# New buffers for gathered rows and one-hot tiles in a fused attention and expert kernel

## The chip, the cores and the metric
The kernel runs on one core of one Trainium2 chip. The metric is the device time of one execution in microseconds (us). The engines are named as the profile names them: PE (matmuls; PEld is its weight load), DVE (vector engine), ACT (scalar engine), POOL (GpSimd), SP (which issues DMAs). Each has its own instruction stream and works it off in order; a wait at the head of a stream holds all that stands behind it.

## The reference
Three stages follow each other. The first is an attention over 32 pooled memory slots per head; its output is read as 4608 tokens of 512 numbers. The second sends each token to one of eight experts of at most 576 tokens, taken greedily by the size of the logit, and applies that expert's two layers. The third is a dense layer pair on all tokens.

```python
a = softmax(phi over the sequence)             # 8 batches, 8 heads, 576 tokens, 32 slots
k_m, v_m = a.T @ k, a.T @ v
x = softmax(q @ k_m.T / 8) @ v_m               # -> 4608 x 512
assigned = greedy(argsort(-(x @ w_gate)), capacity=576)
for e in range(8):
    mask = assigned == e
    out[mask] = relu(x[mask] @ w1[e]) @ w2[e]  # 512 -> 1024 -> 512
h = out @ w_in                                 # 512 -> 2048
y = (h * clip(h + 3, 0, 6) / 6) @ w_out        # 2048 -> 512
```

## The kernel before
**Numbers in halves.** Matmuls run on 16-bit floats. Each factor is split into a high and a low part (scaled by a power of two), and each product is three matmuls. ACT makes the high part, DVE or POOL the low one. The scale needs the largest value over all partitions, which `all_max` finds by a matmul against the identity (tile `amx`, line 694).

**The stages on PE.** After attention, `for P in range(4)` runs `l1(2P)`, `l2(2P)`, `l1(2P+1)`, `l2(2P+1)`, `l34(P)`: the two layers of two experts, and then the dense pair on both experts' 1152 tokens. In `l1` a pass makes a 128-row block of the hidden layer; for expert 0 a pass takes two blocks, 48 matmuls, and there are four passes. `l34` takes 3 chunks of 384 tokens; per chunk it makes 16 hidden tiles (`p<-yt,wi`, 12 matmuls each) and adds 16 products (`acc<-wo,h`, 9 matmuls each), two tiles behind; a group of the latter waits for the `h<-h,p` instruction of its tile on DVE.

**Who fills the gaps.** The engines' orders are fixed when the program is built. A planner written in Python keeps a clock `CK` and estimated times of DVE, ACT and POOL. Background tasks are generators (`routes`, `weights`, `gathers`, `dense`, and the small `ev` tasks that empty a PSUM tile). Each `yield`s the time at which it wants to go on; after every matmul `run()` polls the tasks that are due. `need(cond)` lets the clock run on until a condition holds. So an edit in one task can move instructions of all engines anywhere behind it.

**What the change touches.** `mm_slot` (line 631) deals out the PSUM slots: the list `MMQ` holds the last four, and a new tile waits for the oldest to be emptied. `routes` finds which tokens go to expert k; DVE compares indices into a one-hot tile `OH` of six blocks, six times per expert, and PE multiplies each by `RH` (line 951, `rtp<-RH,OH`, 36 matmuls); the token list `ix` comes out of it. `gathers` fetches an expert's tokens in five blocks `xg` by indirect DMAs on POOL, has PE transpose them (line 623, `xp<-ident,xg`), and writes the two halves `xt`. `weights` loads a layer's weights in four blocks `wst` (indirect DMAs on POOL), finds their scale (the trace prints its maximum as `s_0m` for expert 0 and `s_1m` for expert 1, without the layer; the one at 275.62 us is of the second layer), and splits them: eight instructions each on ACT and DVE (`w<-wst,s,w`). `dense` converts the dense weights, which come as 64-bit floats, in 32 pieces; each takes four DVE instructions on a buffer `cva` (three with two inputs, one with one), some ACT work and one POOL subtraction (`wi<-cva,wi` or `wo<-cva,wo`). `spare` lends these pieces the buffers that nobody uses at the time. The scale of a finished expert's output is `sy_0m` or `sy_1m`.

Of the kernel before, what the change touches and what calls it, by code (L numbers as in the profile page):

```python
# [9 lines left out]
F32 = mybir.dt.float32  # L10
F16 = mybir.dt.float16
BF16 = mybir.dt.bfloat16
# [8 lines left out]
def attn_moe_kernel(ctx: ExitStack, tc: tile.TileContext, q, k, v, phi, w_gate, w1, w2, w_in, w_out, out):  # L21
    nc = tc.nc
    B, H, S, D = q.shape
    M = phi.shape[3]
    E = w_gate.shape[1]
    NT = 36
# [18 lines left out]
    ones_c = consts.tile([128, 128], F32)  # L45
# [44 lines left out]
    with tc.tile_pool(name="ald", bufs=2) as ald, tc.tile_pool(name="aw", bufs=2) as aw, \  # L90
# [3 lines left out]
        for i in range(2):  # L94
            t = slot(26 + i, [128, 4, 2, 64], F32, f"vna{i}")
# [349 lines left out]
        for t in range(-LEAD - 4 - PRE, NTK + A1 + 2):  # L445
# [72 lines left out]
            if t in DT:  # L518
                tag, m = DT[t]
                bufs, shape = (2, [128, 2, 4, R * D]) if tag == "kvt" else (3, [128, H, 4 * D])  # L520
# [25 lines left out]
    rt = ctx.enter_context(tc.tile_pool(name="rt", bufs=1))  # L546
# [33 lines left out]
    V_ = Eng(nc.vector, 0.1, 0.00105)  # L580
# [48 lines left out]
    MMQ = []  # L629

    def mm_slot(done):
        while len(MMQ) >= 4:
            d = MMQ.pop(0)
            b, CK.busy = CK.busy, False
            need(lambda: d[0])
            CK.busy = b
        MMQ.append(done)

    def mm_tile(shape, name, done):
# [22 lines left out]
    nc.vector.tensor_scalar(triu, jp, 0.0, None, op0=OP.is_lt)  # L662
    onesb = rt.tile([128, 128], BF16, name="onesb")
    nc.vector.memset(onesb, 1.0)
    ones72 = rt.tile([128, 2 * NT], F32, name="ones72")
    nc.vector.memset(ones72, 1.0)
    wE = rt.tile([128, E], F32, name="wE")
    nc.vector.tensor_scalar(wE, iT[:, 0:E], -1.0, float(E), op0=OP.mult, op1=OP.add)
    pb = rt.tile([128, 4], F32, name="pb")
# [67 lines left out]
    def route(k):  # L737
# [120 lines left out]
        else:  # L858
# [11 lines left out]
        V_.scalar_tensor_tensor(G[:, 0], V, thf, be, op0=OP.is_gt, op1=OP.mult)  # L870
        V_.scalar_tensor_tensor(G[:, 1], V, thf, be, op0=OP.is_equal, op1=OP.mult)
        sc = rt.tile([128, 2, NT], F32, name="scn")
        V_.tensor_tensor_scan(sc.rearrange("p a t -> p (a t)"), ones72, G.rearrange("p a t -> p (a t)"), 0.0,
                              op0=OP.mult, op1=OP.add)
        tot = rt.tile([128, 2], BF16, name="tot")
        V_.tensor_copy(tot, sc[:, :, NT - 1])
# [46 lines left out]
        p = ps.tile([128, 64], F32, name="rtp")  # L923

        def oh(q4):
            o = rt.tile([128, 6, 128], BF16, name="OH", bufs=3)
            V_.tensor_tensor(o, lo[:, 6 * q4:6 * q4 + 6, None].to_broadcast([128, 6, 128]),
                             i128[:, None, :].to_broadcast([128, 6, 128]), op=OP.is_equal)
            return o
# [53 lines left out]
    def weights():  # L983
        for T in range(2 * E):
            k, which = divmod(T, 2)
            while k not in EIX or T == 3 and 1 not in XI:
                yield CK.now + 0.3
            for c in range(4):
                if T == 0 and c == 2:
                    while not OHP[0]:  # L990
                        yield CK.now + 0.1
                w_issue(T, c)
                yield CK.now + 0.8, G_
            while not XD[0]:
                yield CK.now + 0.1
            sq = rt.tile([128, 4], F32, name="wsq", bufs=2)
            for c in range(4):
                st, ready = WST[T, c]
                yield ready, A_
                scr = wk.tile([128, 1024], BF16, name="wscr")  # L1000
                A_.activation(scr, st, AF.Square, accum_out=sq[:, c:c + 1])
                yield A_.t - 0.3
            s4 = rt.tile([128, 1], F32, name="ws4", bufs=2)
            yield A_.t + HOP
            while 0 not in IDX:
                yield CK.now + 0.1
            V_.tensor_reduce(s4, sq, axis=AX.X, op=OP.add)
            yield V_.t + HOP
            s = yield from pow2(s4, f"s{which}_{k}", True, 0, (4, 13)[which])
            (S1, S2)[which][k] = s  # L1010
            while k and (L1D, L2D)[which].get(k - 1, 0) < (8, 4)[which]:
                yield CK.now + 0.3
            tl, rd = [], []
            for n in range(9):
                if n < 8:
                    c, i = divmod(n, 2)
                    if i == 0:
                        tl.append(wk.tile([128, 2, 1024], F16, name=f"w{which}_{c}"))
                    cs = slice(i * 512, i * 512 + 512)
                    if n in PS.get(T, ()):  # L1020
                        A_.activation(WST[T, c][0][:, cs], WST[T, c][0][:, cs], AF.Copy, scale=s[:, 0:1])
                        yield A_.t - 0.3
                        A_.activation(tl[c][:, 0, cs], WST[T, c][0][:, cs], AF.Copy)
                    else:
                        A_.activation(tl[c][:, 0, cs], WST[T, c][0][:, cs], AF.Copy, scale=s[:, 0:1])
                    rd.append(A_.t + HOP)
                if n and n - 1 in PS.get(T, ()):
                    yield rd[n - 1], G_
                    c, i = divmod(n - 1, 2)
                    cs = slice(i * 512, i * 512 + 512)  # L1030
                    G_.tensor_tensor(tl[c][:, 1, cs], WST[T, c][0][:, cs], tl[c][:, 0, cs], op=OP.subtract)
                    yield CK.now + 0.1, A_
                    WC[T] = c + i, tl
                elif n:
                    yield rd[n - 1], V_
                    c, i = divmod(n - 1, 2)
                    cs = slice(i * 512, i * 512 + 512)
                    V_.scalar_tensor_tensor(tl[c][:, 1, cs], WST[T, c][0][:, cs], s[:, 0:1], tl[c][:, 0, cs],
                                            op0=OP.mult, op1=OP.subtract)
                    if i and T + 1 < 2 * E and T != 2:  # L1040
                        w_issue(T + 1, c)
                    yield CK.now + 0.1, A_
                    WC[T] = c + i, tl
            yield V_.t
            (W1, W2)[which][k] = tl

    XT, XI = {}, set()

    def ybuf(m):
        return wk.tile([128, CAP], F32, name=f"y_{m}")  # L1050
# [4 lines left out]
    def gathers():  # L1055
        for k in range(E):
# [7 lines left out]
            def fetch(i):  # L1064
                n = 64 if i == 4 and k % 2 == 0 else 128
                if k == 0:
                    xg = hbuf(3 + i)[:, 0:512]
                elif k == 1 and i > 1:
                    if i % 2 == 0:
                        big.append(wk.tile([128, 2, 512], F32, name="xg", tag=f"wst{i // 2 - 1}"))  # L1070
                    xg = big[-1][:, i % 2]
                else:
                    xg = wk.tile([128, 512], F32, name="xg", tag=f"xg{i % 2}")
                G_.indirect_dma_start(out=xg[:n], out_offset=None, in_=xd, in_offset=U(ap=ix[:n, i:i + 1], axis=0))
                rdy.append(dma(0.75, G_.t))
                xgs.append((i, n, xg))
            depth = 2 if k > 1 else 5
            big = []
            if k == 0:
                G_.t = max(G_.t, XDT[0])  # L1080
            for i in range(depth):
# [1 line left out]
                    while not SR[0]:  # L1083
                        yield CK.now + 0.1
                fetch(i)
            XI.add(k)
            while k and L1D.get(k - 1, 0) < 8:
                yield CK.now + 0.3
            xt = wk.tile([128, 2, 4, CAP], F16, name="xt")
# [56 lines left out]
    def spare(kind):  # L1146
        tags = ["dst0", "dst1", "dst2"] if kind else ["cva0", "cva1"]
        if 1 in XT or 1 in L1D:
            tags += [] if kind else ["xg0", "xg1"]
        if 1 in W2:  # L1150
            tags += [f"wst{c}" for c in range(4)] if kind else ["wscr"]
        for t in tags:
            if t not in BUSY:
                return t
# [379 lines left out]
```

## Time and profile before
| | us |
|---|---|
| three runs | 1522.28, 1525.7, 1526.74 (median 1525.7) |
| profiled execution | 1519.59 |
| its span | 1517.7 |
| PE busy | 1402.9 (92%) |
| DVE busy | 838.6 (55%) |
| ACT busy | 734.0 (48%) |
| POOL busy | 481.0 (32%) |

All rows below are of the profiled execution, whose own time lies 6.1 us under the median of the three runs. The attention stage takes the first part of the span. `l1(0)` starts at about 255 us, `l2(0)` at 294.04, `l1(1)` at 324.83, `l2(1)` at 350.94, the first `l34` at 381.20; after that PE is nearly always busy. Shares of the span hide this: DVE is busy 55% of the span and nearly all of the time in the stretch where the dense weights are converted.

### The profile page before, as it was taken

Reading aid. Unit: us, or ns where it says so; the run is one execution under the profiler, and the core shown is the slowest. Engines: PE = TensorE matmul, PEld = TensorE weight load, DVE = VectorE, ACT = ScalarE, POOL = GpSimd, SP = SyncE. Lnnn points to the kernel's source line nnn. Section 1 sums busy time; section 2 is a strip of 40 time slices with the busy share of each in tenths; the row PEclk is TensorE's granted clock in tenths of the full one; section 3 lists DMA queues with packets and bytes.
Section 4 is the critical chain, followed back from the end, with each engine's and each line's share of the span. In section 5 each row is a group of like instructions: output and inputs, shape, how many; then the busy total and the mean of one; then the engine's idle time right before and its main releaser. Section 6 shows DMA issues by size and latency. Waiting matters only on the chain.

```text
span 1517.7 us, 26287 instructions
## 1 busy us (share of the span) xinstructions
PE 1402.9 (92%) x10506; PEld 931.7 (61%) x10506; DVE 838.6 (55%) x1985; ACT 734.0 (48%) x1419; POOL 481.0 (32%) x557
## 2 busy tenths in 40 slices
PE   4778886898889999999999999999999999999997
PEld 3667765786444445897544458885545588855553
DVE  5788967899985973453158743522477335221111
ACT  3667655577763553453335533623346536233332
POOL 4555305134552533200224332102235311023232
PEclk9989996999999999999999999999999999999999
DMA  9865577355300420200003220200023102000000
GB/s 301 291 229 194 178 254 242 131 179 167 112 27 22 136 78 21 82 17 1 1 22 93 72 70 30 70 1 1 21 67 111 56 29 70 1 0 22 1 21 21
DMA packets 65913, 130.67 MB, mean 86 GB/s; under 512 B 5248, under 2 KB 35968, under 8 KB 65792
## 3 DMA queue, kind: packets, MB, share of 16 engines
q1 hardware_dynamic: 49808, 74.48, 14.9%
q0 software_dynamic: 15168, 52.96, 10.8%
q8 instruction: 82, 1.34, 0.4%
q10 hardware_dynamic: 816, 1.57, 0.3%
q14 instruction: 39, 0.32, 0.1%
HBM read 110.12 MB, written 18.87 MB: 85 GB/s over the span
## 4 chain that ended last, share of the span: by engine, by line
PE 64%; DVE 16%; issue 6%; ACT 6%; DMA 5%; POOL 3%; SPq 0%; ACTq 0%; POOLq 0%; DVEq 0%
PE p L618 37%; PE acc L618 19%; DVE cva L567 4%; PE xa L420 2%; DMA xg<-xd,ix 2%; DMA wst<-in_moe_w_dram,ei 2%; POOL h L567 1%; DVE h L567 1%; PE kvp L191 1%; PE rtp L794 1%; DMA kvt<-in_v_dram 1%; DVE OH L567 1%; ACT wscr L567 1%; ACT h L567 1%; DVE pm L138 1%
## 5 line engine op out<-in xcount | busy, mean ns | idle before, releaser
L618 PE MATMUL p<-yt,wi 128*128 128x384 f16 x2304 | 422.8, 327 | 0.0
L618 PE MATMUL acc<-wo,h 128*128 128x512 f16 x1728 | 418.0, 380 | 4.5 <-ACT h L567 4.0
L567 POOL TENSOR_TENSOR h<-h,h 128x384 f16<-128x384 f32 x192 | 183.7, 957 | 623.6 <-ACT h L567 449.6
L618 PEld LDWEIGHTS <-w 128*128 128x128 f16 x3072 | 339.6, 121 | 49.9 <-issue 4.3
L618 PEld LDWEIGHTS <-wi 128*128 128x128 f16 x2304 | 218.6, 98 | 155.7 <-issue 1.6
L567 DVE SCALAR_TENSOR_TENSOR h<-h,p 128x384 f32<-128x384 f32 x192 | 105.9, 551 | 332.6 <-ACT h L567 317.1
L567 ACT ACTIVATE h<-p,half_c,inv 128x384 f32<-128x384 f32 (+1 forms) x256 | 143.9, 587 | 301.2 <-PE p L618 293.3
L618 PEld LDWEIGHTS <-h 128*128 128x128 f16 x1728 | 163.7, 98 | 173.7 <-ACT h L567 5.6
L618 PE MATMUL p<-xt,w 128*128 128x288 f16 x1536 | 198.0, 288 | 3.7 <-DVE h L567 3.5
L618 PE MATMUL p<-h,w 128*128 128x288 f16 x1536 | 197.3, 288 | 4.3 <-DVE w L567 3.7
L567 ACT ACTIVATE h<-h 128x384 f16<-128x384 f32 x192 | 100.1, 521 | 117.8 <-DVE h L567 116.5
L567 POOL DMA_INDIRECT wst<-in_moe_w_dram,ei x64 | 66.2, 1035 | 110.2 <-DVE tot L567 33.8
L567 DVE SCALAR_TENSOR_TENSOR h<-p,h 128x288 f16<-128x288 f32 x128 | 57.3, 454 | 78.9 <-ACT h L567 78.9
L567 ACT ACTIVATE h<-p 128x288 f16<-128x288 f32 x128 | 52.1, 414 | 90.7 <-PE p L618 89.7
L567 DVE SCALAR_TENSOR_TENSOR w<-wst,s,w 128x512 f16<-128x512 f32 x124 | 94.5, 781 | 2.4 <-ACT w L567 2.4
L567 ACT ACTIVATE w<-wst,s 128x512 f16<-128x512 f32 x124 | 83.7, 715 | 8.5 <-DVE s L567 5.8
L567 DVE SCALAR_TENSOR_TENSOR cva<-dst,cva 128x512 int32<-128x512 int32 (+1 forms) x96 | 82.6, 881 | 0.4 <-ACT dst L567 0.2
L567 DVE TENSOR_REDUCE ym<-y 128x1 f32<-128x288 f32 x64 | 28.8, 450 | 93.8 <-ACT y L567 91.9
L567 ACT ACTIVATE wscr<-wst 128x1024 bf16<-128x1024 f32 x64 | 67.3, 1052 | 19.0 <-DMA wst<-in_moe_w_dram,ei 18.0
L567 ACT ACTIVATE y<-p 128x288 f32<-128x288 f32 x64 | 26.0, 406 | 96.3 <-PE p L618 92.8
L567 POOL DMA_INDIRECT xg<-xd,ix x35 | 36.4, 1040 | 75.1 <-PE xp L623 55.6
L191 PE MATMUL kvp<-kvt,A 128*64 128x128 f32 x576 | 44.6, 309 | 7.3 <-ACT A L170 3.0
(313 smaller groups left out, 1568.5 us busy)
## 6 DMA issues: line engine op xcount, KB each, us to landing
dst<-in_moe_w_out_dram SPq DMA_DIRECT2D x26, 512.0 KB, 3.6
qt<-in_q_dram SPq DMA_DIRECT2D x8, 1024.0 KB, 13.3
dq<-in_moe_w_in_dram SPq DMA_DIRECT2D x16, 512.0 KB, 4.9
xd<-xs SPq DMA_DIRECT2D x32, 256.0 KB, 5.1
kvt<-in_k_dram SPq DMA_DIRECT2D x7, 1152.0 KB, 5.4
kvt<-in_v_dram SPq DMA_DIRECT2D x7, 1152.0 KB, 12.4
dst<-in_moe_w_in_dram SPq DMA_DIRECT2D x15, 512.0 KB, 4.6
ph<-in_phi_dram SPq DMA_DIRECT2D x8, 576.0 KB, 11.0
```

Of the source, the lines that this page charges most:

```text
L138: nc.vector.tensor_reduce(pm, PH[b].rearrange("p h (r m) -> p h m r", m=M), axis=AX.X, op=OP.max)
L191: nc.tensor.matmul(p[i * 64:(i + 1) * 64, g, 0:128], A[:, hp, r, :], KV[b][:, :, hp, r * 64:(r + 1) * 64], start=(r == 0), stop=(r == R - 1))
L420: nc.tensor.matmul(p[r, g], AT[u][:, half, g, r], VB[b][:, g], start=True, stop=True)
L567: r = f(*a, **kw)
L618: nc.tensor.matmul(o, l, r, start=start, stop=stop)
L794: nc.tensor.matmul(p[:60, :32], C[:, 4 * t:4 * t + 4].rearrange("p t n -> p (t n)"), Bo[:, 4 * t:4 * t + 4].rearrange("p t e -> p (t e)"), ...
```

## The change
Five edits. `mm_slot` waits for the oldest slot first and takes it off the list afterwards; before, it took it off first and waited with three on the list, so that a background task's matmul could take the fourth. `OH` has two buffers instead of three, and a constant tile of ones that only the scan used goes. `xg` has three buffers of its own for all experts but the first; before it had two, and expert 1's third to fifth block lay in the weight buffers `wst0` and `wst1`. So `weights` no longer waits for expert 1's gathers (`XI`) and reloads its buffers at once there too (`T != 2`). The gathers run three blocks ahead for experts 2 to 7 (two before), and three for expert 1 (five before). `spare` may lend `xg2` as well.

```diff
--- before.py
+++ after.py
@@ -630,10 +630,12 @@
 
     def mm_slot(done):
         while len(MMQ) >= 4:
-            d = MMQ.pop(0)
+            d = MMQ[0]
             b, CK.busy = CK.busy, False
             need(lambda: d[0])
             CK.busy = b
+            if MMQ and MMQ[0] is d:
+                MMQ.pop(0)
         MMQ.append(done)
 
     def mm_tile(shape, name, done):
@@ -662,8 +664,6 @@
     nc.vector.tensor_scalar(triu, jp, 0.0, None, op0=OP.is_lt)
     onesb = rt.tile([128, 128], BF16, name="onesb")
     nc.vector.memset(onesb, 1.0)
-    ones72 = rt.tile([128, 2 * NT], F32, name="ones72")
-    nc.vector.memset(ones72, 1.0)
     wE = rt.tile([128, E], F32, name="wE")
     nc.vector.tensor_scalar(wE, iT[:, 0:E], -1.0, float(E), op0=OP.mult, op1=OP.add)
     pb = rt.tile([128, 4], F32, name="pb")
@@ -870,7 +870,7 @@
         V_.scalar_tensor_tensor(G[:, 0], V, thf, be, op0=OP.is_gt, op1=OP.mult)
         V_.scalar_tensor_tensor(G[:, 1], V, thf, be, op0=OP.is_equal, op1=OP.mult)
         sc = rt.tile([128, 2, NT], F32, name="scn")
-        V_.tensor_tensor_scan(sc.rearrange("p a t -> p (a t)"), ones72, G.rearrange("p a t -> p (a t)"), 0.0,
+        V_.tensor_tensor_scan(sc.rearrange("p a t -> p (a t)"), ones_c[:, 0:2 * NT], G.rearrange("p a t -> p (a t)"), 0.0,
                               op0=OP.mult, op1=OP.add)
         tot = rt.tile([128, 2], BF16, name="tot")
         V_.tensor_copy(tot, sc[:, :, NT - 1])
@@ -923,7 +923,7 @@
         p = ps.tile([128, 64], F32, name="rtp")
 
         def oh(q4):
-            o = rt.tile([128, 6, 128], BF16, name="OH", bufs=3)
+            o = rt.tile([128, 6, 128], BF16, name="OH", bufs=2)
             V_.tensor_tensor(o, lo[:, 6 * q4:6 * q4 + 6, None].to_broadcast([128, 6, 128]),
                              i128[:, None, :].to_broadcast([128, 6, 128]), op=OP.is_equal)
             return o
@@ -983,7 +983,7 @@
     def weights():
         for T in range(2 * E):
             k, which = divmod(T, 2)
-            while k not in EIX or T == 3 and 1 not in XI:
+            while k not in EIX:
                 yield CK.now + 0.3
             for c in range(4):
                 if T == 0 and c == 2:
@@ -1037,14 +1037,14 @@
                     cs = slice(i * 512, i * 512 + 512)
                     V_.scalar_tensor_tensor(tl[c][:, 1, cs], WST[T, c][0][:, cs], s[:, 0:1], tl[c][:, 0, cs],
                                             op0=OP.mult, op1=OP.subtract)
-                    if i and T + 1 < 2 * E and T != 2:
+                    if i and T + 1 < 2 * E:
                         w_issue(T + 1, c)
                     yield CK.now + 0.1, A_
                     WC[T] = c + i, tl
             yield V_.t
             (W1, W2)[which][k] = tl
 
-    XT, XI = {}, set()
+    XT = {}
 
     def ybuf(m):
         return wk.tile([128, CAP], F32, name=f"y_{m}")
@@ -1065,17 +1065,12 @@
                 n = 64 if i == 4 and k % 2 == 0 else 128
                 if k == 0:
                     xg = hbuf(3 + i)[:, 0:512]
-                elif k == 1 and i > 1:
-                    if i % 2 == 0:
-                        big.append(wk.tile([128, 2, 512], F32, name="xg", tag=f"wst{i // 2 - 1}"))
-                    xg = big[-1][:, i % 2]
                 else:
-                    xg = wk.tile([128, 512], F32, name="xg", tag=f"xg{i % 2}")
+                    xg = wk.tile([128, 512], F32, name="xg", tag=f"xg{i % 3}")
                 G_.indirect_dma_start(out=xg[:n], out_offset=None, in_=xd, in_offset=U(ap=ix[:n, i:i + 1], axis=0))
                 rdy.append(dma(0.75, G_.t))
                 xgs.append((i, n, xg))
-            depth = 2 if k > 1 else 5
-            big = []
+            depth = 3 if k else 5
             if k == 0:
                 G_.t = max(G_.t, XDT[0])
             for i in range(depth):
@@ -1083,7 +1078,6 @@
                     while not SR[0]:
                         yield CK.now + 0.1
                 fetch(i)
-            XI.add(k)
             while k and L1D.get(k - 1, 0) < 8:
                 yield CK.now + 0.3
             xt = wk.tile([128, 2, 4, CAP], F16, name="xt")
@@ -1146,7 +1140,7 @@
     def spare(kind):
         tags = ["dst0", "dst1", "dst2"] if kind else ["cva0", "cva1"]
         if 1 in XT or 1 in L1D:
-            tags += [] if kind else ["xg0", "xg1"]
+            tags += [] if kind else ["xg0", "xg1", "xg2"]
         if 1 in W2:
             tags += [f"wst{c}" for c in range(4)] if kind else ["wscr"]
         for t in tags:
```

**What it moves.** On PE, the scale matmul `amx<-ident,s_0m` stood between the second and the third pass of `l1(0)`; it now stands one pass later. At the end of `l1(0)`, the order before goes straight from the last `l1` matmul into `l2(0)`, whose matmuls read `h`:

```order
L618 LDWEIGHTS w_3_3652
L618 MATMUL p_4081<-xt,w_3_3652 128x288
L618 LDWEIGHTS w_0_3982
L618 MATMUL p_4172<-h_3678,w_0_3982 128x288
L854 LDWEIGHTS onesb
L854 MATMUL rtp<-ce,onesb 128x8
```

Now routing's matmuls for expert 1 come first: two of its scan, and then the one-hot ones.

```order
L618 MATMUL p_4091<-xt,w_3_3650 128x288
L881 LDWEIGHTS tri
L881 MATMUL rtp<-tot,tri 128x2
L882 LDWEIGHTS triu
L882 MATMUL rtp<-tot,triu 128x1
L951 LDWEIGHTS OH
L951 MATMUL rtp<-RH,OH 128x10
```

24 matmuls `rtp<-RH,OH` stand there, of four `OH` tiles, and behind them the first of `l2(0)`.

On DVE, expert 1's `OH` tiles stood between dense pieces (`cva`) and the maxima `ym` of `l2(0)`'s results:

```order
L567 TENSOR_TENSOR R_4274<-hi,iTf 128x180
L567 TENSOR_TENSOR RH<-R_4274,idt 128x360
L567 TENSOR_TENSOR OH<-lo,i_2717 128x768
L567 SCALAR_TENSOR_TENSOR cva<-dst,cva 128x512
L567 TENSOR_REDUCE ym<-y_4171 128x1
L567 TENSOR_TENSOR OH<-lo,i_2717 128x768
L567 SCALAR_TENSOR_TENSOR cva<-dst,cva 128x512
L567 TENSOR_TENSOR OH<-lo,i_2717 128x768
L567 SCALAR_TENSOR_TENSOR cva<-dst,cva 128x512
L567 TENSOR_REDUCE ym<-y_4282 128x1
L567 TENSOR_TENSOR OH<-lo,i_2717 128x768
```

In the new order they stand between the splits of expert 0's second weight (`w_2`, `w_3`):

```order
L567 TENSOR_TENSOR R_4213<-hi,iTf 128x180
L567 TENSOR_TENSOR RH<-R_4213,idt 128x360
L567 TENSOR_TENSOR OH<-lo,i_2717 128x768
L567 SCALAR_TENSOR_TENSOR w_2_4151<-wst_3673,s_0_3901,w_2_4151 128x512
L567 TENSOR_TENSOR OH<-lo,i_2717 128x768
L567 SCALAR_TENSOR_TENSOR w_2_4151<-wst_3673,s_0_3901,w_2_4151 128x512
L567 TENSOR_TENSOR OH<-lo,i_2717 128x768
L567 SCALAR_TENSOR_TENSOR w_3_4221<-wst_3697,s_0_3901,w_3_4221 128x512
L567 TENSOR_TENSOR OH<-lo,i_2717 128x768
L567 SCALAR_TENSOR_TENSOR w_3_4221<-wst_3697,s_0_3901,w_3_4221 128x512
L567 TENSOR_TENSOR OH<-lo,i_2717 128x768
```

No `ym` stands between them now, since `l2(0)` has not begun. Up to the fourth `OH` there are 5 `cva`, one `w` and 3 `ym` less on DVE than before, counted from the start of the stage.

Also on DVE, the end of the dense conversion, among the hidden tiles of the first `l34`. Before, the last `cva` stood between the 13th and the 14th `h` of 128x384:

```order
L567 TENSOR_SCALAR cva<-dst 128x512
L567 SCALAR_TENSOR_TENSOR cva<-dst,cva 128x512 x4
L567 SCALAR_TENSOR_TENSOR h_5819<-h_5819,p_5792 128x384
L567 SCALAR_TENSOR_TENSOR cva<-dst,cva 128x512
L567 TENSOR_SCALAR cva<-dst 128x512
L567 SCALAR_TENSOR_TENSOR cva<-dst,cva 128x512 x2
L567 SCALAR_TENSOR_TENSOR h_5860<-h_5860,p_5833 128x384
L567 SCALAR_TENSOR_TENSOR cva<-dst,cva 128x512
L567 SCALAR_TENSOR_TENSOR h_5897<-h_5897,p_5874 128x384
L567 SCALAR_TENSOR_TENSOR h_5926<-h_5926,p_5908 128x384
L567 SCALAR_TENSOR_TENSOR h_5954<-h_5954,p_5936 128x384
```

Now it stands between the 10th and the 11th:

```order
L567 TENSOR_SCALAR cva<-dst 128x512
L567 SCALAR_TENSOR_TENSOR h_5763<-h_5763,p_5735 128x384
L567 SCALAR_TENSOR_TENSOR cva<-dst,cva 128x512 x5
L567 SCALAR_TENSOR_TENSOR h_5804<-h_5804,p_5781 128x384
L567 SCALAR_TENSOR_TENSOR h_5840<-h_5840,p_5818 128x384
L567 SCALAR_TENSOR_TENSOR h_5869<-h_5869,p_5851 128x384
L567 SCALAR_TENSOR_TENSOR h_5897<-h_5897,p_5879 128x384
L567 SCALAR_TENSOR_TENSOR h_5925<-h_5925,p_5907 128x384
L567 SCALAR_TENSOR_TENSOR h_5953<-h_5953,p_5935 128x384
```

Ahead of the first `h` instruction of `l1(1)` there are 31 `cva` instead of 21, and 88 instead of 76 ahead of the maximum `sy_1m`; the total of 128 is the same.

## Rows read from the trace of the kernel before
**Rows 1.** Stretch, length; PE, PEld, DVE, ACT, POOL busy (count), PEclk, DMA, GB/s
```profile
274.50:313.90 39.40, 34.47 (x311) 28.11 (x311) 35.52 (x97) 21.19 (x43) 7.97 (x7) 1.00 0.35 119
313.90:328.75 14.85, 12.79 (x103) 10.59 (x101) 13.29 (x31) 9.40 (x17) 9.69 (x9) 1.00 0.55 161
328.75:389.87 61.12, 52.26 (x390) 43.06 (x387) 60.23 (x106) 47.98 (x95) 24.89 (x18) 0.94 0.54 174
389.87:446.32 56.45, 52.00 (x268) 26.35 (x269) 55.74 (x77) 40.47 (x71) 32.00 (x26) 0.97 0.21 66
```

**Rows 2.** The same stretches, `cva` on DVE alone
```profile
274.50:313.90 39.40, 5.70 (x9) 1.00 0.35 119
...
328.75:389.87 61.12, 41.78 (x55) 0.94 0.54 174
389.87:446.32 56.45, 45.30 (x52) 0.97 0.21 66
```

**Rows 3.** PE: start, length, operation, out<-in, tile, count, [idle before <-releaser]
```profile
357.78 23.58 PE L618 MATMUL p<-h,w 128*128 128x288 f16 x169 [2.28 <-DVE w L567]
...
390.17 0.46 PE L694 MATMUL amx<-ident,sy_1m 128*128 128x128 f32 x2 [4.42 <-DVE sy_1m L567]
```

**Rows 4.** DVE in time, dense stage of the first two experts
```profile
433.90 0.54 DVE L567 SCALAR_TENSOR_TENSOR h<-h,p 128x384 f32<-128x384 f32 x1
...
444.66 1.66 DVE L567 SCALAR_TENSOR_TENSOR cva<-dst,cva 128x512 f32<-128x512 f32 x1
```

**Rows 5.** PE in time, dense stage of the first two experts
```profile
435.16 2.10 PE L618 MATMUL acc<-wo,h 128*128 128x512 f16 x9
...
447.81 2.11 PE L618 MATMUL p<-yt,wi 128*128 128x384 f16 x12
449.76 2.10 PE L618 MATMUL acc<-wo,h 128*128 128x512 f16 x9
451.70 2.11 PE L618 MATMUL p<-yt,wi 128*128 128x384 f16 x12
```

**Rows 6.** Waits of transposes, 500 to 1300 us: until what, us, times
```profile
  DMA xg<-xd,ix: 4.5, 6
  DVE w L567: 0.8, 1
```

**Rows 7.** PE in time, l1 and l2 of expert 0
```profile
275.62 0.49 PE L694 MATMUL amx<-ident,s_0m 128*128 128x128 f32 x2 [1.12 <-DVE h L567]
...
290.99 2.43 PE L618 MATMUL p<-xt,w 128*128 128x288 f16 x18
294.04 0.28 PE L618 MATMUL p<-h,w 128*128 128x288 f16 x1 [0.62 <-ACT h L567]
...
324.83 2.12 PE L618 MATMUL p<-xt,w 128*128 128x288 f16 x16
```

**Rows 8.** DVE in time, routing of expert 1 and weights of expert 0
```profile
302.23 1.92 DVE L567 TENSOR_TENSOR OH<-lo,i 128x768 bf16<-128x768 int32 x1
...
306.82 0.95 DVE L567 TENSOR_TENSOR OH<-lo,i 128x768 bf16<-128x768 int32 x1
...
313.93 0.15 DVE L567 COPY ix<-ix 64x1 int32<-64x1 int32 x1
...
316.12 3.39 DVE L567 SCALAR_TENSOR_TENSOR w<-wst,s,w 128x512 f16<-128x512 f32 x5
...
328.75 0.45 DVE L567 SCALAR_TENSOR_TENSOR h<-p,h 128x288 f16<-128x288 f32 x1
```

**Rows 9.** PE from 355 to 365 us, columns as in Rows 1
```profile
355.00:365.00 10.00, 7.72 (x42) 0.66 0.84 300
```

**Rows 10.** POOL in time: a subtraction, and gathers of expert 2
```profile
302.18 1.16 POOL L567 TENSOR_TENSOR wi<-cva,wi 128x512 f16<-128x512 f32 x1 [2.14 <-PE rtp L951]
...
511.80 1.10 POOL L567 DMA_INDIRECT xg<-xd,ix  x1 [0.30 <-issue]
...
514.91 1.17 POOL L567 DMA_INDIRECT xg<-xd,ix  x1 [1.08 <-DMA xg<-xd,ix]
```

## The prediction
> **What bounds the kernel now.** I read the sums by stretch first, then the vector engine and the matmul engine in order of time, then the instruction order of both kernels. The place that matters is the time from 274 to 450 us, where the first two experts run and the dense weights are still being converted on DVE (tile `cva`, four instructions per piece, 32 pieces). From 274.5 to 446.3 us DVE is busy for 164.8 of 171.8 us; it idles 3.88, 1.56, 0.89 and 0.71 us in the four stretches, 7.04 us in all [rows 1]. In the last two of them, `cva` alone takes 41.8 and 45.3 us, 0.76 and 0.87 us each [rows 2]. So here DVE sets the pace, and PE waits for it: 2.28 us for an expert weight `w`, 4.42 us for the scale `sy_1m` [rows 3]. The stretch ends when DVE has issued its last `cva` at 444.66 us, over at 446.32 [rows 4]; PE then runs its dense stage at its own pace, 1.95 us for a hidden tile `p` and 1.94 for an `acc` group [rows 5]. A dense `acc` group starts about 1.26 us after the `h<-h,p` instruction of its hidden tile on DVE (433.90 to 435.16) [rows 4, 5]. After 450 us PE is nearly never without work, and what is left there of this change are the waits for gathered rows: 4.5 us over experts 2 to 7 [rows 6].
>
> **The change, part by part.**
> The slot queue (`mm_slot`). Before, its oldest entry was popped ahead of the wait, so a background task could slip a matmul in. The row shows what that cost and gave: the maximum for the first expert's second weight (`amx<-s_0m`) held PE for 1.12 us at 275.62 [rows 7]. Now the task waits for a free slot: in the order the same matmul stands one whole l1 pass later, behind `w_3` of the next pass. So the scale comes about 9 us later (a pass is 48 of the 192 l1 matmuls of 255 to 293 us), and the eight splits of that weight on DVE come late too. In the order, the planner lets routing of expert 1 run ahead meanwhile, and 24 of its 36 one-hot matmuls now stand on PE ahead of the first l2 matmul. They need the fourth `OH` of DVE. Before, that one ended at 306.82+0.95 = 307.77 us [rows 8]. Ahead of it, the new order has on DVE 5 `cva` less (0.63 each [rows 2]: 3.2), one `w` less (0.68 [rows 8]), 3 small maxima `ym` less (some 0.45 each, the length of an `h` row [rows 8]: 1.3), but about 1.6 us more of small work, and the `OH` that took 1.92 instead of 0.95 us loses its reason (1.0). That is 4.6 us less: fourth `OH` at 303.2 us, if DVE waits as often as before in the routing chain. PE finished l1 at 293.4 and began l2 at 294.04 [rows 7]. It will now stand, but for small matmuls, until 303.2: l2 begins 9.2 us late.
>
> l2 of expert 0. It lasted 324.83-294.04 = 30.8 us [rows 7]. Now only 12 one-hot matmuls are left in it and the index is ready about 6 us earlier (before: 313.93 [rows 8]), so its own waits shrink by up to 3 us. Against that stands the clock: around the wait of 2.28 us that ended at 357.78 [rows 3], PE's granted clock was 0.66 over the ten us from 355 to 365, that is two thirds of the time at 1.2 GHz instead of 2.4 [rows 9], which loses 3.4 us of full-speed work. I take 1.0 us off in sum: l1 of expert 1 begins about 8.2 us late, at 333. DVE meets the same lateness, because rows that need PE (the `ym` maxima and the five gathered blocks `xt`) and the scale of the next weight now stand in its queue behind PE's late l2; ACT's `y` copies stand in front of the squares that this scale is made of. So the first `h` of that l1 on DVE, at 328.75 before [rows 8], moves to about 337.3, +8.5 us.
>
> The dense pieces. With three `xg` buffers lent to `spare` and the output weight's scale known earlier, DVE's order has the conversion further ahead. Counted in the order, 31 `cva` instead of 21 stand before that first `h`, 88 instead of 76 before `sy_1m`, and the last one stands ahead of the 11th dense `h<-h,p`, no longer between the 13th and the 14th. From the first `h` to the end, 10 `cva` fall away: +2 up to `sy_1m` at 0.76, -12 after it at 0.87, and three dense `h` at 0.54 [rows 2, 4]: +1.5-10.4-1.6 = -10.5 us. DVE's last `cva` then ends at 446.3+8.5-10.5 = 444.3 us. But only then can the 11th `acc` group go, at 444.3+1.2 = 445.5, and the 14th three groups of 3.89 us later, at 457.2. Before, the 14th began at 449.76 [rows 5]. The first stage therefore loses **7.4 us**.
>
> The bound from below needs no estimate of waits: if DVE idled nowhere from 274.5 us on, it would end at 446.3-7.0-1.6 = 437.7, and the 14th group would start at 450.6, +0.8 us. From above, with 14 us of idle time instead of my 8 to 9, it is +13.
>
> The second expert's own rows and weights. The weight loads of expert 1's second layer go ahead of the transposes' end, and the wait of 2.28 us for `w` [rows 3] goes. It is worth nothing, as DVE is late next: PE will reach the dense stage near 381 us, as now, and wait for `sy_1m` some 14 us instead of 4.42.
>
> Three gather buffers for experts 2 to 7. The third gather was issued at 514.91, 1.08 us of it a wait for the first block to be used [rows 10]; it can now follow the second at once, and the fourth and fifth come one round earlier, at the price that POOL puts one dense subtraction behind a gather issue (1.1 us [rows 10], beside PE's work). Of the 4.5 us [rows 6] the even experts' share goes, while the odd ones still wait for their fourth and fifth rows, whose issues hang on the first transposes as before: I take **-2.5 us**, between -5.3 (all of it, and follow-up waits) and +1.
>
> The rest. One set of ones and one one-hot buffer less: a memset gone where DVE waits, the scan reads another constant, and a third `OH` must wait for PE to have used the first, which in the new order it does at once. 0, within 0.5 us each way.
>
> Sum: +7.4-2.5 = **+5 us**. The profiled execution took 1519.6 us and the median is 1525.7; added to the median, 1530.7.
>
> A weighing of one rule. The `OH` at 302.23 took 1.92 us while a POOL subtraction ran from 302.18; the next took 0.95 [rows 8, 10]. The Trainium skill (SBUF — State Buffer, Who interferes with whom) says that VectorE and GpSimd share a pair of ports, which one instruction with two SBUF inputs takes for its whole length. By that rule a `cva` has no length of its own, and the three POOL subtractions fewer before DVE's end give back their whole time; the second rival works this out.
>
> **Rivals.**
> 1. *Faster.* The routing's head start is not lost behind the late l2: DVE finds `cva` work in every gap, idles under 3 us, and POOL's subtractions fall into its waits. Then the first stage gains nothing and loses nothing (+0.8 at no idle time), all 5.3 us of gather waits go: 1525.7-4.5 = 1521.2. For it: the pieces are further ahead in the order. Against: in-order rows that need PE stand between them. It decides from about 2 us of idle time on. 0.20.
> 2. *The port.* Three POOL subtractions less before DVE's last `cva`, at the mean 1.23 us of 32.00 us in 26 [rows 1], take 3.7 us off the 7.4: +3.7-2.5 = +1.2, 1526.9. For it: the pair 1.92 and 0.95. Against: mean `cva` of 0.76 and 0.87 differ little with and without dense `h` work. 0.20.
> 3. *Slower by more.* PE's near-standstill from 293 to 303 us keeps the low clock through half of l2, and DVE waits for everything in it: 14 us of idle time, +13-2.5, about 1536. For it: [rows 9]. Against: PE came back within those ten us there. 0.15.
> 4. *The layout doesn't do what it says*: gathers were hidden behind l2 anyway and the early loads behind DVE, the slot order shifts work both ways: within 2 us, 1526. 0.10.
>
> **How the numbers follow.** My forecast has 0.35, with a range of its own from 1527 to 1537. 0.3% of the time is 4.6 us, about what a measurement of this kernel can tell from none. Slower by more than that: two thirds of the forecast, all of the third rival, and a bit of the second and fourth, 0.45; faster: most of the first rival and little else, 0.20; the rest, 0.35. The range for 8 in 10 takes in the first rival's centre and the third's: 1520.5 to 1538.
>
> **What would show it.** Right: PE stands from about 293 to 303 us waiting for `OH`, with a low clock behind it; l1 of expert 1 begins near 333; PE waits over 10 us for `sy_1m`; the last `cva` ends near 444 and the 14th `acc` group starts near 457; the waits for `xg` after 500 us sum to about 2 us. Wrong: l2 of expert 0 beginning before 298, or the last `cva` ending before 437; and if the waits for `xg` stay at 4.5 us, the gather term is nought.

## The result, and the profile after

| | us |
|---|---|
| before, median of 6 runs | 1526.22 (1521.42 to 1528.29) |
| changed, median of 6 runs | 1534.76 (1532.40 to 1537.35) |
| ratio, changed to before | 1.0077, 95% interval 1.0057 to 1.0097 |
| profiled execution of the changed kernel | 1534.92, span 1533.2 |

The changed kernel is slower by 0.77% of 1526, or 11.7 us. That is the estimate from all runs of both kernels; the two medians as they stand lie 8.5 us apart. The two profiled executions lie 15.3 us apart. 2.55 us of that stand ahead of everything the change reorders: `l1(0)` begins at 257.49 us instead of 254.94. So times of the two traces are compared below from the start of `l1(0)`, and what is left there is 12.9 us. In those terms `l2(0)` begins 8.0 us later than before, `l1(1)` 10.4, `l2(1)` 10.0, the first `l34` 12.45, its 14th `acc` group 12.5, and the last matmul 12.9. On PE the whole lag is there when the dense stage starts; it grows between the end of `l1(0)` and that start.

PE of the changed kernel in time, with the rows that answer to [rows 3, 5, 7] (start, length, operation, count, idle time before it and what ended it):

```profile
286.05 0.49 PE L694 MATMUL amx<-ident,s_0m 128*128 128x128 f32 x2 [0.88 <-DVE h L567]
...
299.82 0.32 PE L951 MATMUL rtp<-RH,OH 128*128 128x10 bf16 x6 [4.60 <-DVE OH L567]
...
304.41 0.32 PE L951 MATMUL rtp<-RH,OH 128*128 128x10 bf16 x6 [1.21 <-DVE OH L567]
304.59 2.56 PE L618 MATMUL p<-h,w 128*128 128x288 f16 x10
...
317.58 0.66 PE L623 MATMUL xp<-ident,xg 128*128 128x128 f32 x4 [1.31 <-DMA xg<-xd,ix]
...
325.45 0.63 PE L623 MATMUL xp<-ident,xg 128*128 128x128 f32 x4 [1.80 <-DMA xg<-xd,ix]
...
337.77 3.72 PE L618 MATMUL p<-xt,w 128*128 128x288 f16 x29
...
367.27 0.91 PE L618 MATMUL p<-h,w 128*128 128x288 f16 x6 [2.30 <-DVE w L567]
370.12 1.62 PE L618 MATMUL p<-h,w 128*128 128x288 f16 x6 [1.94 <-DVE w L567]
372.81 23.55 PE L618 MATMUL p<-h,w 128*128 128x288 f16 x169 [1.07 <-DVE w L567]
...
396.20 5.69 PE L618 MATMUL p<-yt,wi 128*128 128x384 f16 x34
...
406.43 0.77 PE L694 MATMUL amx<-ident,sy_1m 128*128 128x128 f32 x2 [4.55 <-DVE sy_1m L567]
...
464.78 2.11 PE L618 MATMUL acc<-wo,h 128*128 128x512 f16 x9
```

The maximum `s_0m` runs at 286.05; from the start of `l1(0)` that is 28.6 us, before it was 20.7. PE then waits for one-hot tile after one-hot tile and begins `l2(0)` at 304.59. `l2(0)` lasts 33.2 us instead of 30.8, with waits for gathered rows at 317.58 and 325.45. In `l2(1)` there are now three waits for `w`, 5.3 us, where before there were two, 3.7 us. From the start of `l34` to the 14th group it is 68.6 us in both traces. The rows of the kernel before, as far as they were not shown yet:

```profile
317.65 0.64 PE L623 MATMUL xp<-ident,xg 128*128 128x128 f32 x4 [1.03 <-DMA xg<-xd,ix]
...
354.59 0.91 PE L618 MATMUL p<-h,w 128*128 128x288 f16 x6 [1.41 <-DVE w L567]
```

DVE of the changed kernel, for [rows 4, 8]:

```profile
303.40 0.95 DVE L567 TENSOR_TENSOR OH<-lo,i 128x768 bf16<-128x768 int32 x1
304.27 0.75 DVE L567 SCALAR_TENSOR_TENSOR w<-wst,s,w 128x512 f16<-128x512 f32 x1
...
310.53 0.15 DVE L567 COPY ix<-ix 64x1 int32<-64x1 int32 x1
...
313.93 0.45 DVE L567 TENSOR_REDUCE ym<-y 128x1 f32<-128x288 f32 x1 [0.89 <-ACT y L567]
316.35 0.43 DVE L567 TENSOR_SCALAR cva<-dst 128x512 int32<-128x512 int32 x1 [1.97 <-POOL wi L567]
...
319.75 0.69 DVE L567 SCALAR_TENSOR_TENSOR cva<-dst,cva 128x512 f32<-128x512 f32 x1 [1.52 <-ACT dst L567]
...
340.92 0.45 DVE L567 SCALAR_TENSOR_TENSOR h<-p,h 128x288 f16<-128x288 f32 x1
...
347.59 0.43 DVE L567 TENSOR_SCALAR cva<-dst 128x512 int32<-128x512 int32 x1 [2.04 <-DMA dst<-in_moe_w_in_dram]
...
447.18 4.50 DVE L567 SCALAR_TENSOR_TENSOR cva<-dst,cva 128x512 int32<-128x512 int32 x5
451.60 0.55 DVE L567 SCALAR_TENSOR_TENSOR h<-h,p 128x384 f32<-128x384 f32 x1
```

The fourth `OH` is followed by the last split of `w_3` (304.27), so PE and weights become ready together. The last `cva` ends at 447.18+4.50 = 451.68. Between 313 and 320 us DVE stands three times: for `y` of the late `l2(0)`, for POOL to give a `cva` buffer back, and for a dense piece on ACT. The longest single wait comes later, 2.04 us for a dense load at 347.59 (4.09 us in the second trace of this kernel); before, no wait of DVE for a dense load was over 0.2 us.

POOL and the DMA engines at the gathers of expert 1, first before, then changed. The window rows go from the index `ix` on DVE to PE's first transpose (columns as in Rows 1):

```profile
314.16 0.97 POOL L567 DMA_INDIRECT xg<-xd,ix  x1 [3.49 <-DVE ix L567]
...
313.93:317.65 3.72, 2.70 (x23) 1.95 (x21) 3.69 (x10) 3.03 (x6) 2.88 (x3) 1.00 0.46 117
```

```profile
310.08 0.94 POOL L567 DMA_INDIRECT wst<-in_moe_w_dram,ei  x1 [0.30 <-issue]
311.32 0.95 POOL L567 DMA_INDIRECT xg<-xd,ix  x1 [0.30 <-DVE cva L567]
...
310.53:317.58 7.05, 5.74 (x47) 4.35 (x46) 4.01 (x9) 3.42 (x6) 4.86 (x5) 1.00 0.95 321
```

Four loads of expert 1's first weight (`wst`) need the buffers that the splits of expert 0's second weight give back. Before, POOL issued them 40 to 44 us after `l1(0)` began, 15 us ahead of the first gather. With the late splits it issues them at 45 to 53 us, and the first gather follows the last of them at once. From the index to PE's first transpose the DMA engines are then busy for 0.95 of the time, instead of 0.46, and it takes 7.05 us instead of 3.72. That the loads delay the rows is read from these rows; no run moved the loads alone.

The stretches of [rows 1], cut in the changed kernel at the matching instructions, with the time around the standstill behind them (columns as in Rows 1):

```profile
277.05:303.40 26.35, 16.51 (x149) 13.99 (x148) 24.18 (x72) 9.90 (x20) 2.20 (x2) 0.87 0.21 61
303.40:337.30 33.90, 29.05 (x229) 22.33 (x230) 25.65 (x53) 20.49 (x37) 17.76 (x15) 0.90 0.53 167
337.30:406.40 69.10, 57.98 (x428) 47.56 (x425) 66.72 (x120) 53.75 (x103) 28.00 (x22) 0.92 0.52 169
406.40:451.60 45.20, 42.86 (x213) 21.61 (x214) 45.03 (x61) 32.01 (x57) 25.18 (x20) 0.93 0.17 54
...
299.00:304.60 5.60, 1.16 (x25) 0.90 (x26) 5.60 (x8) 0.00 (x0) 0.96 (x1) 0.50 0.08 8
304.60:310.00 5.40, 5.40 (x40) 3.53 (x37) 4.15 (x9) 1.35 (x2) 4.18 (x2) 0.50 0.66 196
```

DVE idles 2.17, 8.25, 2.38 and 0.17 us: 12.97 in all, 7.03 before. That does not make its end later by as much: DVE has 3.1 us less work up to its last `cva` (161.7 instead of 164.8), which ends 2.8 us later than before. Behind it, up to the 14th `acc` group, it is 13.1 us instead of 3.4, since three more dense groups stand there in the order. PE's clock is 0.50 (1.2 GHz) from 299 to 310 us, where the kernel before had 1.00.

`cva` alone ([rows 2]):

```profile
277.05:337.30 60.25, 12.53 (x20) 0.89 0.39 120
337.30:406.40 69.10, 46.73 (x63) 0.92 0.52 169
406.40:451.60 45.20, 35.20 (x40) 0.93 0.17 54
```

0.74 and 0.88 us each, against 0.76 and 0.87. The waits of the transposes ([rows 6]):

```profile
  DMA xg<-xd,ix: 3.3, 6
```

POOL at the gathers of expert 2 ([rows 10]):

```profile
527.33 0.95 POOL L567 DMA_INDIRECT xg<-xd,ix  x1 [0.30 <-issue]
529.38 1.24 POOL L567 DMA_INDIRECT xg<-xd,ix  x1 [0.16 <-DMA xg<-xd,ix]
```

The third gather goes 0.30 us behind the second, instead of 1.08 us behind a landing; now the fourth waits.

### The profile page after: what moved, and what is told of

Same layout as the page of the kernel before. It is cut to its first block, busy times and chain, and to the rows that moved or that the text cites. A ratio compares the mean times of both kernels' runs of the same rounds, so it can differ in the third digit from the quotient of the medians.

```text
span 1533.2 us, 26307 instructions
## 1 busy us (share of the span) xinstructions
PE 1407.7 (92%) x10506; PEld 933.0 (61%) x10506; DVE 839.2 (55%) x1984; ACT 734.4 (48%) x1419; POOL 484.1 (32%) x559
## 4 chain that ended last, share of the span: by engine, by line
PE 67%; DVE 18%; DMA 5%; issue 5%; ACT 3%; POOL 2%; ACTq 0%; SPq 0%; POOLq 0%; DVEq 0%
PE p L618 39%; PE acc L618 19%; DVE cva L567 4%; PE xa L420 2%; DMA xg<-xd,ix 2%; DVE w L567 1%; DVE OH L567 1%; DMA ph<-in_phi_dram 1%; DMA wst<-in_moe_w_dram,ei 1%; DVE h L567 1%; PE kvp L191 1%; PE rtp L794 1%; POOL h L567 1%; DVE pm L138 1%; DVE yt L567 1%
## 5 line engine op out<-in xcount | busy, mean ns | idle before, releaser
L567 POOL TENSOR_TENSOR h<-h,h 128x384 f16<-128x384 f32 x192 | 179.2, 934 | 630.6 <-ACT h L567 456.8
L567 POOL DMA_INDIRECT wst<-in_moe_w_dram,ei x64 | 74.2, 1159 | 145.1 <-DVE w L567 39.4
L567 ACT ACTIVATE y<-p 128x288 f32<-128x288 f32 x64 | 26.1, 407 | 104.2 <-PE p L618 103.0
```

The costliest lines, as they stand in the source:

```text
L567: r = f(*a, **kw)
```

## The experiments

Each was timed beside the kernel before on the same chip, where that one's median was 1521.6 or 1521.7 us. A ratio is to the kernel before and is the estimate from all runs of both, with its 95% interval; the quotient of the two medians differs from it by up to 0.26%.

**The slot edit undone.** The changed kernel with

```diff
-            d = MMQ[0]
+            d = MMQ.pop(0)
             b, CK.busy = CK.busy, False
             need(lambda: d[0])
             CK.busy = b
-            if MMQ and MMQ[0] is d:
-                MMQ.pop(0)
```

> The changed kernel with mm_slot as before; all new buffers stay. Theory S (the slot edit costs the time: the scale of expert 0's second weight is late, so l2(0) begins late): l2(0) begins 39 us after l1(0), as before (47 in the changed kernel), and the time is that of before less the 1.2 us of gather waits: 1525. Rival L (the new layout costs it: expert 1's early loads collide with the dense loads, DVE waits 2.0 us for a dense load and 2.0 for POOL): l2(0) begins at 39 us too, but expert 1's weight waits stay at 5.3 us and the time at 1532 to 1535.

Ratio 1.0002 (0.9981 to 1.0022). `l2(0)` begins 38.95 us after `l1(0)` (259.26). PE in `l2(0)` and `l2(1)`:

```profile
298.21 0.28 PE L618 MATMUL p<-h,w 128*128 128x288 f16 x1 [0.60 <-ACT h L567]
...
361.73 23.68 PE L618 MATMUL p<-h,w 128*128 128x288 f16 x192
...
396.91 0.77 PE L692 MATMUL amx<-ident,sy_1m 128*128 128x128 f32 x2 [6.62 <-DVE sy_1m L567]
```

`l2(1)` has no wait for `w` any more: 192 matmuls in one row of 23.68 us, where before they took 30.3 with two waits. So the new layout does what it says for expert 1, and it is worth nothing that can be measured (0.2% to either side): PE then waits 6.6 us for `sy_1m` instead of 4.4, and `l2(0)` and `l1(1)` took 6.6 us longer together (34.2 and 29.3 instead of 30.8 and 26.1), with waits of 2.4 us for `sy_0m` and 1.8 for `s_1m`. DVE's waits for a dense load and for POOL are gone too. Theory S holds, rival L falls.

**One matmul alone.** The changed kernel, with one exception in `all_max`; `WT` is raised while `mm_slot` waits:

```diff
-        while len(MMQ) >= 4 and not MMQ[0][0]:
+        ok = nm in ('s1_0',)
+        while len(MMQ) >= 4 and not MMQ[0][0] and not (ok and WT[0]):
             yield CK.now + 0.05
+        if len(MMQ) >= 4 and ok and WT[0] and not MMQ[0][0]:
+            MMQ.pop(0)
```

> The changed kernel with one exception: the maximum for expert 0's second weight (amx<-s_0m) may take the place of a slot that is being waited for, as before; every other tile waits as in the change. In the order this brings back the place of that one matmul, of the one-hot matmuls and of l2(0). If that one matmul is the cause: l2(0) begins 39 us after l1(0), ratio to before 1.000 (as with the whole of the old mm_slot). If the other slots matter: half of the loss stays, ratio 1.003 or more.

Ratio 1.0016 (0.9998 to 1.0035). From `l1(0)` to 250 us behind it, the orders of PE, DVE, ACT and POOL are those of the kernel with the old `mm_slot`, instruction for instruction; DVE's and ACT's first differ near 645 us of the trace. `l1(0)` begins at 256.84, `l2(0)` 39.8 us later:

```profile
296.66 0.28 PE L618 MATMUL p<-h,w 128*128 128x288 f16 x1 [0.62 <-ACT h L567]
```

So the place of this one matmul brings back the whole order of the stage, and 0.61% of the 0.77%. The interval holds 1.000 as well as 1.003, so the time alone does not decide between the two forecasts; if the other slots cost something, it is behind this stage.

**Late scale, but `l2` first.** The changed kernel with `l2` asking block by block:

```diff
-            need(lambda: k in W2)
...
+                    need(lambda: k in W2 or WC.get(2 * k + 1, (0,))[0] > j // 2)
                     for wi, xi in ((0, 0), (0, 1), (1, 0)):
-                        mm(p, W2[k][j // 2][:, wi, j % 2 * 512 + m * 128:j % 2 * 512 + m * 128 + 128], HT[k][j][:, xi, cs], n == 0, n == 23, fp16(288))
+                        mm(p, WC[2 * k + 1][1][j // 2][:, wi, j % 2 * 512 + m * 128:j % 2 * 512 + m * 128 + 128], HT[k][j][:, xi, cs], n == 0, n == 23, fp16(288))
```

> The changed kernel, but l2 asks for each of its four weight blocks when it needs it, not for all of them ahead; in the order l2(0) now stands ahead of expert 1's one-hot matmuls, while the scale stays late. Theory P (the place of the one-hot matmuls on PE costs the time): l2(0) begins 40 us after l1(0), the 8 us come back, 1526. Theory W (the late splits cost it: w_3 is ready on DVE only at about 305 us in the changed kernel): l2(0) begins at 40 us, but waits inside its first pass for w_2 and w_3, some 5 us in sum; 1531, and l1(1) begins 5 us earlier than in the changed kernel at most.

Ratio 1.0013 (0.9998 to 1.0029). PE, with `l1(0)` at 260.60:

```profile
298.49 0.90 PE L618 MATMUL p<-h,w 128*128 128x288 f16 x6 [1.11 <-DVE h L567]
...
302.93 0.32 PE L951 MATMUL rtp<-RH,OH 128*128 128x10 bf16 x6 [2.75 <-DVE OH L567]
...
367.31 23.49 PE L618 MATMUL p<-h,w 128*128 128x288 f16 x175 [3.58 <-DVE w L567]
```

`l2(0)` begins 37.9 us after `l1(0)`, stands for a one-hot tile inside its first pass (not for `w_2` or `w_3`, as Theory W had it), and is 36.8 us long. `l1(1)` begins 5.6 us earlier than in the changed kernel; Theory W had 5 at most there and 1531 for the time, Theory P 1526; with 2 us of loss, P is a little nearer in the time, and neither is right in the whole. The waits for `w` in `l2(1)` stay, 5.3 us.

**Early scale, but `l2` held.** The slot edit undone, and

```diff
-            need(lambda: k in W2)
+            need(lambda: k in W2 and OHN[0] >= 4)
```

where `OHN` counts expert 1's one-hot tiles multiplied.

> The changed kernel with mm_slot as before, and l2(0) held back in the order until four one-hot tiles of expert 1 are multiplied: scale and splits early, one-hot matmuls ahead. Theory P: l2(0) begins 47 to 48 us after l1(0) and the end moves with it: 1533. Theory W: the held time lets DVE convert 7 pieces of 0.75 us more ahead of l1(1) than in the kernel without the hold, which come back in the dense stage: 1528 to 1529.

Ratio 1.0024 (1.0007 to 1.0040). PE, with `l1(0)` at 261.67:

```profile
308.04 0.33 PE L949 MATMUL rtp<-RH,OH 128*128 128x10 bf16 x6 [4.34 <-DVE OH L567]
...
313.59 3.28 PE L618 MATMUL p<-h,w 128*128 128x288 f16 x13
...
372.53 23.77 PE L618 MATMUL p<-h,w 128*128 128x288 f16 x192
```

`l2(0)` begins 51.9 us after `l1(0)`, 4.8 us later than in the changed kernel, and yet the loss is a third of the changed kernel's: with the scale early, DVE splits and converts in the meantime, and `l2(1)` runs without a wait. Theory W holds here.

**PE kept busy in the standstill.** The changed kernel with 36 idle matmuls ahead of the first one-hot group of expert 1 and 16 behind each of three:

```diff
+        def warm(n):
+            for i in range(n):
+                nc.tensor.matmul(pd, onesb, onesb, start=(i == 0), stop=(i == n - 1))
```

> The changed kernel with 84 idle matmuls (ones by ones, 128x128, results unused) on PE among the one-hot matmuls of expert 1, where PE stood from 295 to 304 us and its clock was 0.50 from 299 to 310. Theory C (the low clock behind the standstill is part of the loss): the clock is near 1.0 from 300 to 310, l2(0) lasts 2.7 us less (5.4 us at half speed), ratio 1.006 instead of 1.0077. Theory D (DVE sets the pace of l2(0)): the clock rises, l1(1) begins when it did, ratio 1.0077.

Ratio 1.0070 (1.0044 to 1.0096). The clock where `l2(0)` starts (PE, PEld, DVE, ACT, POOL):

```profile
301.50:307.00 5.50, 5.50 (x59) 4.24 (x56) 5.40 (x15) 2.04 (x4) 4.26 (x3) 1.00 0.61 194
```

and PE around it:

```profile
301.48 1.39 PE L618 MATMUL p<-h,w 128*128 128x288 f16 x10
...
315.72 1.09 PE L623 MATMUL xp<-ident,xg 128*128 128x128 f32 x4 [4.98 <-DMA xg<-xd,ix]
```

The clock is 1.00 instead of 0.50, PE does more matmuls, and then waits 4.98 us for the gathered rows. `l2(0)` lasts 33.9 us, no less than in the changed kernel, and `l1(1)` begins 81.1 us after `l1(0)` instead of 80.3. So in the trace the full clock brings nothing forward, and Theory C falls there; the time alone (1.0070) could not tell its 1.006 from 1.0077. Theory D is right in the result, but what PE waits for is gathered rows, not DVE.

**Three gather buffers alone.** The kernel before with `xg{i % 3}` and depth 3 for experts 2 to 7, two `OH` buffers, and without `ones72`:

```diff
-                    xg = wk.tile([128, 512], F32, name="xg", tag=f"xg{i % 2}")
+                    xg = wk.tile([128, 512], F32, name="xg", tag=f"xg{i % 3}")
...
-            depth = 2 if k > 1 else 5
+            depth = 3 if k > 1 else 5
```

> The kernel before with three gather buffers for experts 2 to 7 (two one-hot buffers and the other constant to make room); expert 1 as before, mm_slot as before. The order of the first two experts is that of before. If the gather term is what the changed kernel's trace shows: waits of the transposes for xg 3.3 us instead of 4.5, time 1525, within 0.1% of before. If it is the forecast's 2.5 us: waits near 2, time 1523.7. If depth gives nothing: 4.5 us and 1526.

Ratio 0.9991 (0.9971 to 1.0011). The transposes waited 2.1 us for `xg`, 5 times:

```profile
  DMA xg<-xd,ix: 2.1, 5
```

The waits are near the forecast's 2 us; the time, 1.4 us less, can't be told from no change. It is the fastest kernel of all here, by less than it can be measured.

**The changed kernel again.** No edit.

> The changed kernel itself beside the others, for a second trace and the same company: 1.0077 of before, l2(0) 47 us after l1(0), l2(1) 32.7 us long with 5.3 us of waits for w.

Ratio 1.0075 (1.0051 to 1.0099). `l2(0)` begins 47.6 us after `l1(0)`, `l2(1)` lasts 31.9 us with 5.3 us of waits for `w`. The transposes waited 2.4 us for `xg`. The clock in the first 5.6 us of `l2(0)` was low again:

```profile
306.40:312.00 5.60, 5.60 (x40) 3.67 (x40) 4.23 (x9) 1.35 (x2) 4.23 (x3) 0.50 0.68 199
```

**What they have in common.** For each kernel, DVE's busy and idle time from the same place (19.56 us after `l1(0)` begins) to the end of its last `cva`, read from the stretches' sums as above. The last `cva`, the 14th `acc` group and the end are in us after `l1(0)`, all of the one traced execution; the ratio is of all runs:

| kernel | `l2(0)` after `l1(0)` | DVE busy | DVE idle | last `cva` ends | 14th group | end | ratio |
|---|---|---|---|---|---|---|---|
| before | 39.1 | 164.8 | 7.0 | 191.4 | 194.8 | 1262.8 | 1 |
| slot edit undone | 39.0 | 164.5 | 7.0 | 191.1 | 197.4 | 1264.7 | 1.0002 |
| one matmul alone | 39.8 | 165.5 | 7.2 | 192.3 | 198.6 | 1268.6 | 1.0016 |
| gather buffers alone | 38.8 | 163.4 | 8.0 | 191.0 | 195.5 | 1263.5 | 0.9991 |
| early scale, `l2` held | 51.9 | 163.1 | 9.4 | 192.0 | 202.2 | 1268.7 | 1.0024 |
| late scale, `l2` first | 37.9 | 163.2 | 9.7 | 192.4 | 198.7 | 1268.8 | 1.0013 |
| changed | 47.1 | 161.7 | 13.0 | 194.2 | 207.3 | 1275.7 | 1.0077 |
| changed, second trace | 47.6 | 163.0 | 14.3 | 196.9 | 210.0 | 1280.4 | 1.0075 |
| PE kept busy | 47.2 | 161.6 | 15.4 | 196.5 | 209.6 | 1278.3 | 1.0070 |

DVE's work varies by 4 us, its idle time by 8, and the three slow rows are the three with 13 us or more. Those three have one order, though (the last with the idle matmuls added). In this stretch the gather buffers alone have the order of the kernel before, and one matmul alone has that of the slot edit undone, so the table holds five orders; two traces of one order differ by 0.2 to 1.4 us of idle time. Idle time goes with the slow rows, but it moves only the end of the last `cva`. The rest of the lag at the 14th group is what the order leaves to PE behind that end. Two of the stretches' sums, of the kernel with the slot edit undone and of the changed kernel's second trace (DVE alone):

```profile
278.82:450.36 171.54, 164.51 (x305) 0.97 0.39 125
```

```profile
278.42:455.73 177.31, 162.99 (x305) 0.91 0.38 121
```

Neither half of the cause is dear by itself. A held `l2(0)` with an early scale costs 0.24% (0.07 to 0.40), a late scale with `l2(0)` in front 0.13% (0.29 at most), both together 0.77% (0.57 to 0.97). Whether the two simply add is not shown. By the ratios they fall short, but in the traces, from `l1(0)` to the end, the halves cost 5.9 and 6.0 us and the changed kernel 12.9 and 17.6; and the traced executions of the halves took 6.6 and 7.3 us more than the medians of their kernels.

## Why the prediction was right, and which terms were off

It forecast a loss of 5 us, from the slot edit and by way of DVE, and the loss is 11.7 us (8.7 to 14.8), more than twice as much. The direction and the path were right, and both ranges hold 1534.76; the size was not. Of the signs named ahead, PE's stand for `OH` with a low clock behind it came, and `l1(1)` near 333 (335.2 on that scale); the wait for `sy_1m`, the last `cva`, the 14th group and, in the first trace, the waits for `xg` missed. Point by point, times from the start of `l1(0)`:

- **The late scale and `l2(0)`.** Forecast: the scale about 9 us late, `l2(0)` 9.2 late. Measured 7.9 and 8.0 (8.5 in the second trace); the first `h` of `l1(1)` on DVE moved by 9.6 us (340.92 less 328.75 and 2.55), forecast 8.5. Right, and putting that one matmul back brings `l2(0)` and most of the time back.
- **`l2(0)` itself.** Forecast 1.0 us shorter, measured 2.4 longer (1.9 in the second trace). The index was 6 us earlier, as forecast (310.53 against 313.93, less the 2.55), but the first rows reached PE 7.1 us behind it (317.58 less 310.53) instead of 3.7 (317.65 less 313.93). The prediction had the index early, but not what comes to stand ahead of the gathers: the late splits put four weight loads there, with the DMA engines 0.95 busy. The low clock, which the forecast named, was hidden by that wait, as the busy PE shows.
- **DVE up to the last `cva`** is the term that was mis-sized. From the first `h` of `l1(1)` on, the sum took off 10.5 us, and 6.8 came off (117.6 to 110.8 us). The ten `cva` less are there and gave what was forecast. But the 16 `yt` (the scaled tokens for the dense stage) took 14.1 us instead of 12.0, three small instructions of the scale `sy_0` joined (0.6 us), and DVE idled 0.9 us more. With the first `h` 1.1 us later than forecast, the last `cva` ends at 449.1 instead of 444.3 (451.68 less the 2.55), and the 14th group starts at 462.2 instead of 457.2.
- **Its idle time.** The text says 8 to 9 us; its sum (444.3 against 437.7 with none) holds 6.6, and by the same sum 14 us would be +14.8, not +13. It was 13.0, and 14.3 in the second trace, with 1.5 us less work than the sum had: +12.5 at the 14th group, near the upper bound named.
- **The place of the last `cva`.** Right: ahead of the 11th `h`. The lead of 10 to 12 pieces in the order gave nothing back in time: the last `cva` ends 2.8 us later, and the three groups behind it take 13.1 us up to the 14th, close to the 12.9 of the sum (457.2 less 444.3).
- **The wait of 2.28 us for `w`.** Forecast: it goes and is worth nothing. With the slot edit it does not go: three waits for DVE's splits, 5.3 us. Without the slot edit it goes, and is worth nothing. So PE reached the dense stage at 396.20, not near 381, and waited 4.55 us for `sy_1m`, not 14: this step of the forecast was wrong.
- **The gathers.** Forecast -2.5 us, on waits down from 4.5 to about 2. The waits came down to 3.3 and 2.4 in the two traces, to 2.1 with the buffers alone (2.8 and 3.5 with the slot edit undone and with one matmul alone). A gain in time is not shown: that kernel's -1.4 us has an interval of 3 us to either side, and from the 14th group to the end the traces take 1068.0 us before, 1068.0 with the buffers alone, 1068.4 and 1070.5 in the changed kernel. So this term misses the same way as the first.
- **The rivals.** The port's 3.7 us did not come. Up to the last `cva`, POOL runs one subtraction and three `h` less than before, where the forecast counted three subtractions. `cva` took 94.5 us in the stretch (the sum of its three rows above), 1.1 less than before. The effect itself is large in both traces: a `cva` with two inputs takes 0.67 to 0.73 us with no POOL instruction beside it but a DMA issue, and up to 1.66 with one. Against the lengths without POOL that is some 33 us of DVE's busy time before and some 32 after (an estimate from the traces: each instruction less the median of its form with no POOL beside it). The rule of the Trainium skill (SBUF — State Buffer, Who interferes with whom), by which the two engines lock each other out of a shared pair of ports, agrees with these lengths, as with those weighed in the prediction. But the POOL instructions that are left meet DVE nearly as often, so about 1 us is all that changed. The third rival had the price right (about 1536) and DVE's idle time too; the clock that it blamed was not the reason.

Not settled: `l1(0)` began between 254.3 and 261.7 us in the seven traces with the new layout, and at 254.9 and 253.3 in the two with the old one. In the trace of the changed kernel a store of attention's output held ACT for 3.49 us near 190 us, but ACT's waits for that store come to 6.3 us there and to 6.8 before (165 to 225 us), and to 4.5 in the trace with the latest start, so they do not explain it. Whether the layout does it or chance was not tried; with the slot edit undone, the layout as a whole costs 0.22% at most.

## What to carry to other kernels

In a program whose order a planner fixes, an edit of a few lines to a resource rule (who may take a slot while another waits) can outweigh the buffers that it comes with; compare the orders and look for the one small instruction, here a maximum, on which a chain of work depends. Where one engine sets the pace of a stretch, count its idle time: moves that leave its work as it is cost what they add to its idle time, and what they leave to the next engine behind its last instruction. A wait that vanishes on PE was worth nothing here while DVE ended last. And when weights become ready later, ask which loads their buffers release later, and what those then stand in front of.

## What was not expected of the hardware

A clock of 0.50 over 11 us cost nothing that could be measured, because the gathered rows came no sooner: at full clock PE waited 4.98 us for them, in the changed kernel 1.31 and 1.80. From the index to the first transpose it took 3.72 us with the DMA engines 0.46 busy, and 7.05 us with four weight loads issued just ahead and the DMA engines 0.95 busy. And where POOL ran beside them, DVE's instructions were longer, by an estimated 33 of DVE's 165 busy us in this stretch, yet four POOL instructions less brought back only about 1 us.
